# An mLSTM cell with a leaky-ReLU feed-forward on one core: the fourth w_in quarter narrowed ahead of step 5's scores, two q loads asked for first, six spare products

## The chip, the core and the metric

The kernel runs on one core of a Trainium2 chip. A core has a matrix engine (TensorE, PE in the profile, with its weight loads as PEld), a vector engine (VectorE, DVE), an activation engine (ScalarE, ACT), GpSimd (POOL) and SyncE (SP), which here only asks for DMA transfers. The metric is the device time of one execution in microseconds, lower is better; a time is the median of several runs.

## What is computed

```python
# q, k, v, o_gate: (4, 8, 768, 40) float32; i_gate, f_gate: (4, 8, 768)
for t in range(S):
    m_new = np.maximum(f_gate[:, :, t] + m, i_gate[:, :, t])
    f_stab = np.exp(f_gate[:, :, t] + m - m_new)
    i_stab = np.exp(i_gate[:, :, t] - m_new)
    m = m_new
    C = f_stab[:, :, None, None] * C + i_stab[:, :, None, None] * np.einsum('bhd,bhe->bhde', vt, kt)
    n = f_stab[:, :, None] * n + i_stab[:, :, None] * kt
    h_tilde = np.einsum('bhde,bhe->bhd', C, qt)
    nq = np.einsum('bhd,bhd->bh', n, qt)[:, :, None]
    denom = np.maximum(np.abs(nq), 1.0)
    y[:, :, t] = 1.0 / (1.0 + np.exp(-o_gate[:, :, t])) * h_tilde / denom
# (batch, head, seq, dim) -> x of (3072, 320); w_in (320, 2048), w_out (2048, 320)
h = x @ w_in
g = np.maximum(0.01 * h, h)
return (g @ w_out).astype(np.float32)
```

Both weights arrive as float64, so the kernel reads them as pairs of 32-bit words and narrows them to float32 itself.

## The kernel before

The sequence is cut into six chunks of 128 tokens. A step is one chunk of one of the four batches: step s is chunk s // 4, batch s % 4, so steps 0 to 3 are chunk 0, steps 4 to 7 chunk 1. Inside a chunk the recurrence is written as matrix products: scores of keys against queries, weighted by an exponential of gate sums, and a state carried from one chunk to the next. The feed-forward of a chunk runs on TensorE between the cell's products of the next chunk.

**The order is written out by hand** for TensorE, VectorE, ScalarE and GpSimd: the Python calls give each of these engines its queue in order. Each works its queue strictly in turn, so an instruction that waits holds up everything behind it on its engine. Only SyncE's queue is laid out by the planner.

**Chunk 0** is `first_chunk()`. It loads k, q, v and the output gates of steps 0 to 3, makes the scores (`u_scores`, sc), multiplies them into the weights w on VectorE (L594), forms the values (`u_values`, pa: 16 records of 41 columns for a step) and the gated output (`gate`), and transposes it into xT (`u_x`, xt). `warm(n)` (L346) is a helper that multiplies the identity by itself n times into a PSUM tile that nobody reads; chunk 0 begins with two such calls. The first two units of the feed-forward's first product (ph, L790) stand in the same function, the others in the loop behind it. All small PSUM tiles of chunk 0 and of the cell come from one pool of four buffers in turn (`psc`), those of the feed-forward from another four (`psf`).

**Weights.** w_in is loaded in four quarters (n = 0 to 3), w_out in eight blocks (n = 4 to 11) of 640 KB each (`load_weights`). Narrowing one takes six passes in a row: ScalarE L243 and L245, VectorE L247, ScalarE L251, VectorE L253 and L257 (`narrow_weights`; quarters 0 and 1 are done in halves by `narrow_part`, L273 to L287). `now` is a generator over the passes of n = 2 to 11, and the loop of chunk 1 takes a few of them at each index i.

**The loop of chunk 1** has 30 units of feed-forward work, of chunk 0's tokens: for i = 0 to 13 a first product of 256 tokens (ten pairs of records in ph, then its Prelu, L798, which frees its two PSUM banks); for i = 14 to 29 a quarter of an output product (po, L825), quarter m needing the w_out blocks 4 + 2m and 5 + 2m. Units 0 and 1 use w_in quarter n=0, 2 to 5 n=1, 6 to 9 n=2, and 10 to 13 the last quarter, n=3. Around these units `place` sets the cell's parts: for step 4 `u_parts` behind i=2 and `u_plain` behind i=5, for step 5 behind i=7 and i=10, for step 6 behind i=12 and i=15, for step 7 behind i=18 and i=21.

- `u_parts(s)`: transposes of the scaled q (`split_qs`, tq, L550), then the scores (sd, L644) and the state's update (L649) in turn; VectorE multiplies scores by w (L654), which needs the exponentials of `prep_exp` (ScalarE L488), and adds the state (L626).
- `u_plain(s)`: the output gate's tanh (L524), the values (hN, L695), denominators (L663 to L665), the gating (L706, POOL L711) and the second state update.
- `ahead(s)`, called behind the part before: `u_split(s)` transposes k and q of step s (tk, L564, copied by ScalarE at L570), then POOL scales q (`prep_qs`, L517), multiplies the state (L622) and scales k (`prep_vu`, L508). `prep_mask` (POOL L479) adds the mask to w, which a DMA has spread over the partitions (L437).
- `feed(s)` asks for k (L380), four pieces of v (L383) and two of w (L437); `load_late(s, 1)` for q and `load_late(s, 2)` for the output gate (L406, into the tiles rb, two in turn). `fetch` says behind which index the loads of w_out's later blocks (L229) are asked for.

Of the kernel before, what the change touches and what calls it, by code (L numbers as in the profile page):

```python
# [21 lines left out]
def kernel(  # L22
# [133 lines left out]
    def prepare_step(n):  # L156

        nc.gpsimd.memset(S_v[n][:SL, 0, :, :, DB:], 2.0)
        nc.gpsimd.memset(S_v[n][SL:, 1, :, :, DB:], 2.0)
        nc.gpsimd.memset(S_t[n][QW:SL, 1], 0.0)  # L160
# [240 lines left out]
    def load_late(s, i):  # L401

        if B <= s < 2 * B:
            if i > 0:
                c, b = divmod(s, B)
                nc.sync.dma_start(natural(s, i), (k, q, o_gate)[i][b, :, ts(c, P), :].rearrange("h p d -> p h d"))  # L406
        elif s < NS:
            load_blocks(s, i)
# [266 lines left out]
    def gate(s, eng=None):  # L675

        d = st[s]
        d["x"] = wk.tile([P, Dm], F32, name="x")
        x3 = d["x"][:].rearrange("p (h d) -> p h d", d=D)
        nc.vector.scalar_tensor_tensor(  # L680
            x3, in0=d["o"].rearrange("p (h d) -> p h d", d=D), scalar=1.0, in1=d["pa"][:, :, :D],
            op0=ALU.add, op1=ALU.mult,
        )
        (eng or nc.gpsimd).tensor_tensor(x3, x3, d["den"][:].unsqueeze(2).to_broadcast([P, H, D]), op=ALU.mult)
# [78 lines left out]
    def u_x(s, copy=nc.scalar.copy):  # L763

        c, b = divmod(s, B)
        d = st[s]
        if b == 0:
            st["xT", c] = wk.tile([P, KC, GT], F32, name="xT", bufs=1)
        xT = st["xT", c]
        xt = psc.tile([P, KF + 1, P], F32, name="xt", tag="c")  # L770
        for kk in range(KF):
            nc.tensor.transpose(xt[:, kk, :], d["x"][:, ts(kk, P)], ident[:])
        nc.tensor.transpose(xt[:KR, KF, :], d["x"][:, KF * P :], ident[:])
        tok = ts(b, P)
        copy(xT[:, :KF, tok], xt[:, :KF, :])
        copy(xT[:DP, KF + 1 :, tok], xt[DP:, :KF, :])
        copy(xT[DP:, KF : 2 * KF, tok], xt[:DP, :KF, :])
        copy(xT[:DP, KF, tok], xt[:DP, KF, :])
        copy(xT[DP:, 2 * KF, tok], xt[:DP, KF, :])
        if s >= B:  # L780
            del st[s]
# [108 lines left out]
    def feed(s):  # L890
        load(s)
        spread(s)

    def first_chunk():

        tensor_copy = nc.vector.tensor_copy
        for n in range(NL):
            nc.gpsimd.memset(S_t[n][:, 1, :, D:], 2.0)
            nc.gpsimd.memset(S_t[n][SL:, 0], 0.0)
        nc.scalar.activation(first[:], zeros[:], AF.Exp)  # L900
        nc.vector.tensor_copy(ident_b[:], ident[:])
        keys, values = slice(0, 2), slice(2, 3)
        load(0, keys)
        load(1, keys)
        load(0, values)
        load(1, values)
        load_o(0)
        load_o(1)
        load(2, keys)
        load(3, keys)  # L910
        load(2, values)
        load(3, values)
        load_weights(0, (0,))
        load_o(2)
        load_o(3)
        load_weights(1, (0,))
        warm(5)
        spread_mask(0)
        warm(2)
        gates(0)  # L920
        gates_exp(0)
        load_fi(2)
        bu, a, _ = bus[0]
        spread_first(a, 0)
        gates_T(0, bu)
        gates(1)
        run(prep_exp(0))
        u_transpose(0, tensor_copy)
        prep_vu(0)
        u_transpose(1, tensor_copy)  # L930
        u_scores(0)
        run(prep_exp(1))
        prep_vu(1)
        u_scores(1)
        u_state(0, tensor_copy)
        u_state(1, tensor_copy)
        gates_exp(1)
        prep_o(0)
        prep_o(1)
        spread_mask(2)  # L940
        spread_first(a, 2)
        run(prep_exp(2))
        load_weights(0, (1,))
        u_values(0)
        gate(0)
        u_values(1)
        gate(1)
        run(prep_exp(3))
        u_transpose(2)
        u_x(0, tensor_copy)  # L950
        u_scores(2)
        u_transpose(3, tensor_copy)
        u_x(1)
        prepare_step(0)
        prep_vu(2)
        prep_vu(3)
        load_weights(1, (1,))
        prepare_step(1)
        parts = [narrow_part(n, e) for n in range(2) for e in range(2)]
        u_scores(3)  # L960
        run(parts[0], 5)
        u_values(2)
        prep_o(2)
        prep_o(3)
        run(parts[0])
        gate(2, nc.vector)
        u_values(3)
        gate(3, nc.vector)
        run(parts[1], 5)
        ffs = ff_units(0)  # L970
        ffs[0]()
        u_x(2)
        run(parts[1])
        u_x(3, tensor_copy)
        u_state(2, nc.scalar.copy)
        u_state(3, nc.scalar.copy)
        run(parts[2], 1)
        ffs[1]()
        run(parts[2])
        u_gates(1)  # L980
        prepare_tiles()
        prepare_step(2)
        prepare_step(3)
        return ffs, parts[3]

    E = mybir.EngineType
    with tc.manual_schedule(engines={E.PE, E.DVE, E.Activation, E.Pool}):
        ffs, part = first_chunk()
        for s in (B, B + 1):
            feed(s)  # L990
            for i in range(1, 3):
                load_late(s, i)
            load_weights(s - B + 2)
        for n in range(3):
            load_weights(QN + n)
        for s in (B + 2, B + 3):
            feed(s)


        ffs = ffs[2:]  # L1000
        fetch = {5: (3, 4), 9: (5, 6), 16: (7,)}
        place = (2, 5, 7, 10, 12, 15, 16, 18, 21, 22, 24, 26, 28)
        late = {}
        masks = {0: (2, 3), 12: (4, 5)}
        pairs = (2, 2, 6, 6, 14, 14, 19, 19, 19)
        now = (None for n in range(2, QN + NF // 2) for _ in narrow_weights(n))
        for c in range(1, NB + 1):
            if c > 1:
                ffs = ff_units(c - 1)
            cells = cell_units(c) if c < NB else []  # L1010
            n_ff, n_c = len(ffs), len(cells)
            done = fed = 0
            waiting = []
            for i in range(n_ff):
                if c == 1:
                    run(now, (0, 0, 0, 3, 3, 0, 2, 2, 2)[i] if i < 9 else 3 if i < 14 else 4)
                    for n in fetch.get(i, ()):
                        load_weights(QN + n)
                for s, steps in lazy.items():
                    if s in late and late[s] > 0:  # L1020
                        late[s] -= 1
                    else:
                        run(steps, 3)
                for n in masks.get(i, ()) if 1 < c < NB else ():
                    if c * B + n < NS:
                        prep_mask(c * B + n)
                ffs[i]()
                if c == 1 and i == 0:
                    run(part)
                    prep_mask(B)  # L1030
                    ahead(B)
                    load_fi(3)
                if c + 1 < NB:
                    if i == (1 if c == 1 else 0):
                        gates(c + 1)
                    if i == (3 if c == 1 else 2):
                        gates_exp(c + 1)
                upto = min(n_c, sum(p <= i for p in (place if c == 1 else pairs)))
                while done < upto:
                    fn, s = cells[done]  # L1040
                    fn(s)
                    done += 1
                    if fn is u_mix:
                        waiting.append(s)
                    if fn is u_plain and s < 2 * B - 1 or fn is u_parts and s == 2 * B - 1:
                        ahead(s + 1)
                    elif fn is u_mix:
                        ahead(s + 2)
                    elif fn is u_plain:
                        prep_mask(s + 2)  # L1050
                        ahead(s + 2)
                if i >= n_ff // 2 - 1:
                    for s in waiting:
                        gather_x(s)
                    waiting.clear()
                while fed < done:
                    fn, s = cells[fed]
                    fed += 1
                    if fn in (u_mix, u_plain):
                        load_late(s + NR, 2)  # L1060
                        if s + NL < NS:
                            feed(s + NL)
# [31 lines left out]
```

## Time and profile before

| | us |
|---|---|
| median of 3 runs | 527.77 |
| lowest and highest | 527.13, 530.59 |
| the profiled execution | 527.16 |
| its span, first to last instruction | 525.3 |
| TensorE busy | 512.1 |
| VectorE, ScalarE, GpSimd busy | 204.9, 187.8, 108.1 |
| mean granted TensorE clock | 0.98 |

The span is cut by the page into 40 slices of 13.1 us. The digits are busy tenths; the row PEclk is the clock that TensorE was granted, in tenths. The row DMA shows the transfer engines:

```profile
DMA  9999968997635526575526665526532112000000
```

A group's row in the lists that follow gives the line, the engine, what is written and read, the number of instructions, the busy time and the idle time of the engine before them. A row of the timeline gives the start in us, the length, and in brackets the idle time before it with what ended it. A row of the chain of waits gives start, length and the work.

```profile
44.01 0.31 PE L564 MATMUL tk<-ident,kn 64*40 64x64 f32 x4
46.18 0.25 PE L564 MATMUL tk<-ident,rb 64*40 64x64 f32 x2 [1.86 <-DMA rb<-in_q_dram]
...
79.76 4.64 PE L790 MATMUL ph<-xT,w_in 64*128 64x256 f32 x20 [3.58 <-DVE w_in L257]
```

### The profile page before, as it was taken

The numbers are of one execution on the slowest core, as the hardware profiler recorded it, in microseconds if no ns is written. First come the engines' busy times: TensorE is split into PE (matmuls) and PEld (weight loads), VectorE is DVE, ScalarE is ACT, GpSimd is POOL, SyncE is SP. The second block draws the span as 40 slices with busy tenths as digits, with TensorE's granted clock in tenths as the row PEclk, the third lists the DMA queues.
The fourth block names the chain that finished last, engine by engine and source line by source line (L and its number), as shares of the span: only waits on it lengthen the run. The fifth ranks groups of instructions, "written<-read, shape, count | busy, mean of one in ns | idle before, by whom it ended". The sixth has DMA issues, their size and how long they took to land.

```text
span 525.3 us, 11276 instructions
## 1 busy us (share of the span) xinstructions
PE 512.1 (97%) x4495; PEld 333.1 (63%) x4495; DVE 204.9 (39%) x400; ACT 187.8 (36%) x477; POOL 108.1 (21%) x149
## 2 busy tenths in 40 slices
PE   8998979999999999999999999999999999999997
PEld 6787867777554577554577554577554577544674
DVE  6666434587039355039355039354037240000000
ACT  5568894977525122125112125112125100122100
POOL 4453223235005021026021026021013010000000
PEclk9878997999999999999999999999999999999999
DMA  9999968997635526575526665526532112000000
GB/s 122 147 190 164 239 142 200 197 165 152 164 72 117 137 72 159 133 153 119 133 74 151 136 136 130 135 82 160 126 89 64 46 44 87 14 0 1 12 12 25
DMA packets 164419, 59.12 MB, mean 113 GB/s; under 512 B 128432, under 2 KB 155632, under 8 KB 164368
## 3 DMA queue, kind: packets, MB, share of 16 engines
q1 hardware_dynamic: 163408, 56.31, 50.4%
q0 software_dynamic: 576, 1.97, 2.0%
q8 instruction: 35, 0.57, 0.5%
q10 hardware_dynamic: 384, 0.13, 0.1%
q14 instruction: 16, 0.13, 0.1%
HBM read 51.68 MB, written 6.70 MB: 111 GB/s over the span
## 4 chain that ended last, share of the span: by engine, by line
PE 87%; SPq 5%; DMA 3%; DVE 2%; ACT 1%; issue 1%; POOL 1%; ACTq 0%; POOLq 0%
PE po L825 40%; PE ph L790 38%; SPq L378 3%; PE pT L725 3%; PE sd L644 3%; DMA rb<-in_q_dram 1%; DMA acts<-in_moe_w_in_dram 1%; PE sd L649 1%; PE hN L695 1%; PE tk L564 1%; PE tq L550 1%; DVE w_in L257 1%; SPq L383 1%; DMA S<-in_v_dram 0%; SPq L392 0%
## 5 line engine op out<-in xcount | busy, mean ns | idle before, releaser
L790 PE MATMUL ph<-xT,w_in 64*128 64x512 f32 (+1 forms) x1120 | 220.4, 546 | 3.8 <-DVE w_in L257 3.6
L825 PE MATMUL po<-w_out,acts 128*128 128x320 f32 x768 | 211.1, 434 | 0.0
L825 PEld LDWEIGHTS po<-w_out,acts 128*128 128x128 f32 x768 | 144.4, 190 | 62.6 <-issue 3.8
L790 PEld LDWEIGHTS ph<-xT,w_in 64*128 64x128 f32 x1120 | 111.2, 194 | 98.5 <-issue 87.5
L798 ACT ACTIVATE acts<-ph 128x512 f32<-128x512 f32 (+1 forms) x112 | 53.6, 531 | 149.4 <-PE ph L790 149.4
L654 DVE TENSOR_TENSOR qn<-w,sd 64x512 f32<-64x512 f32 x40 | 27.4, 684 | 115.9 <-PE sd L649 61.5
L479 POOL TENSOR_TENSOR w<-w,i 128x512 f32<-128x512 f32 x20 | 27.8, 1394 | 120.8 <-DMA w<-a_dr 85.4
L622 POOL TENSOR_TENSOR S<-S,f 40x336 f32<-40x336 f32 x36 | 28.5, 792 | 115.0 <-PE pT L725 68.3
L488 ACT ACTIVATE w<-w,gT 128x64 f32<-128x64 f32 x160 | 41.2, 339 | 0.0
L833 ACT COPY y<-po 128x320 f32<-128x320 f32 x12 | 5.1, 425 | 84.2 <-PE po L825 84.2
L833 ACT COPY hn<-po 128x320 f32<-128x320 f32 x12 | 5.1, 425 | 76.9 <-PE po L825 76.9
L541 DVE TENSOR_TENSOR qn<-kqT,ea 64x512 f32<-64x512 f32 x32 | 27.0, 843 | 0.9
L732 DVE STREAM_TRANSPOSE hb<-pT 128x512 f32<-128x512 f32 x16 | 11.4, 714 | 39.1 <-PE pT L725 38.9
L739 POOL TENSOR_TENSOR xb<-xb,den 128x320 f32<-128x320 f32 x16 | 11.6, 727 | 66.7 <-DVE xb L736 66.7
L644 PEld LDWEIGHTS sd<-kqT 40*64 40x64 f32 x640 | 19.8, 135 | 6.1 <-issue 6.1
L644 PE MATMUL sd<-kqT 40*64 40x64 f32 x640 | 21.2, 220 | 0.0
L743 DVE STREAM_TRANSPOSE x<-xb 128x512 f32<-128x512 f32 x16 | 18.0, 1122 | 7.7 <-POOL xb L739 7.7
L535 DVE STREAM_TRANSPOSE kqT<-rb 128x512 f32<-128x512 f32 x32 | 20.4, 680 | 0.0
L649 PE MATMUL sd<-S,vu 64*40 64x42 f32 x576 | 20.1, 215 | 0.0
L649 PEld LDWEIGHTS sd<-S,vu 64*40 64x40 f32 x576 | 18.6, 111 | 0.0
L626 DVE TENSOR_TENSOR S<-S,sd 40x336 f32<-40x336 f32 x36 | 18.1, 503 | 1.0
L725 PEld LDWEIGHTS pT<-qn,S 128*64 128x64 f32 x512 | 15.6, 138 | 3.6 <-issue 3.5
(138 smaller groups left out, 348.4 us busy)
## 6 DMA issues: line engine op xcount, KB each, us to landing
w<-a_dr SPq DMA_DIRECT2D x40, 128.0 KB
rb<-in_k_dram SPq DMA_DIRECT2D x64, 80.0 KB
rb<-in_q_dram SPq DMA_DIRECT2D x64, 80.0 KB
rb<-in_o_gate_dram SPq DMA_DIRECT2D x64, 80.0 KB
ea<-a_dr SPq DMA_DIRECT2D x32, 128.0 KB
kn<-in_k_dram SPq DMA_DIRECT2D x24, 160.0 KB
raw<-in_moe_w_out_dram SPq DMA_DIRECT2D x6, 640.0 KB
S<-in_v_dram SPq DMA_DIRECT2D x80, 40.0 KB
```

Of the source, the lines that this page charges most:

```text
L479: nc.gpsimd.tensor_tensor(w, w, cm2.unsqueeze(1).to_broadcast([P, H, SL]), op=ALU.add)
L488: yield nc.scalar.activation(w[:, h, :], of, AF.Exp, bias=gT[c][:, 0, bh : bh + 1], scale=1.0)
L535: nc.vector.transpose(d["kqT"][:, i].rearrange("p (h t n) -> p h n t", n=TS, t=QW), raw_blocks(s, i, QW).rearrange("p (h n) d -> p h n d", ...
L541: nc.vector.tensor_tensor(mixed(s)[rows, 1 - r], d["kqT"][rows, 1].rearrange("p (h t) -> p h t", t=SL), d["ea"][rows], op=ALU.mult,)
L622: nc.gpsimd.tensor_tensor(new, old, g, op=ALU.mult)
L644: nc.tensor.matmul(bank[1 - u][toks, h, :], lhsT=kqT[rows, 0, ts(h, SL)], rhs=kqT[rows, 1, ts(h, SL)], start=True, stop=True,)
L649: nc.tensor.matmul(dC[u][:, h].rearrange("p k d -> p (k d)"), lhsT=d["ku"][toks, h], rhs=S_v[s % NL][toks, u, h, :, :V1], start=True, stop ...
L654: nc.vector.tensor_tensor(mixed(s)[toks, u], w[toks], bank[1 - u][toks], op=ALU.mult)
L725: nc.tensor.matmul(pT[DP * r : DP * (r + 1), j * P + u * SL : j * P + (u + 1) * SL], lhsT=S[:, u, h, :], rhs=m[:, u, h, :], start=True, st ...
L790: nc.tensor.matmul(ph[r][:, cols], lhsT=w_row(r, slot, j), rhs=xT[DP * r : DP * (r + 1), slot, cols], start=(slot == 0), stop=(slot == KC ...
L798: nc.scalar.activation(acts[:, f, cols], ph[r][:, cols], AF.Prelu, alpha=0.01)
L825: nc.tensor.matmul(po[n][:], lhsT=acts[:, f, ts(n, P)], rhs=w_out[:, f, :], start=(f == 0), stop=(f == NF - 1),)
```

## The change

Two calls of `warm` are put into chunk 0, four products ahead of step 3's scores and two between the values of steps 2 and 3. For steps 4 and 5 the q load goes ahead of k, v and w. In the loop of chunk 1 the passes of n=3 are taken three at a time at i = 6 and 7, where they were two at a time at i = 6, 7 and 8, and all later passes follow one index earlier; the loads in `fetch` at 9 and 16 move to 8 and 15.

```diff
         u_scores(2)
         u_transpose(3, tensor_copy)
         u_x(1)
+        warm(4)
         prepare_step(0)
...
         run(parts[0])
         gate(2, nc.vector)
+        warm(2)
         u_values(3)
         gate(3, nc.vector)
...
         for s in (B, B + 1):
+            load_late(s, 1)
             feed(s)
-            for i in range(1, 3):
-                load_late(s, i)
+            load_late(s, 2)
             load_weights(s - B + 2)
...
-        fetch = {5: (3, 4), 9: (5, 6), 16: (7,)}
+        fetch = {5: (3, 4), 8: (5, 6), 15: (7,)}
...
                 if c == 1:
-                    run(now, (0, 0, 0, 3, 3, 0, 2, 2, 2)[i] if i < 9 else 3 if i < 14 else 4)
+                    run(now, (0, 0, 0, 3, 3, 0)[i] if i < 6 else 3 if i < 14 else 4)
```

On VectorE this puts L253 and L257 of n=3 ahead of step 5's L654 and L626. On ScalarE it puts L243 and L245 of n=4 ahead of the Prelu of unit i=8, and so on for the later blocks. In SyncE's queue q of step 4 and of step 5 each moves up past seven entries, and two of the 640 KB loads of w_out, which had two pieces of k of step 9, the two of w of step 8 and one of ea (L445) between them, become neighbours.

## The prediction

> **What bounds the kernel now.** I read the page first: the busy digits by slice, the chain and the groups with their idle time. TensorE is busy in all of the span but a few places.
>
> ```profile
> PE   8998979999999999999999999999999999999997
> PEclk9878997999999999999999999999999999999999
> ```
>
> Every digit below 9, of busy share and of clock, lies in the first seven slices of 13.1 us, up to about 92 us. Behind them TensorE runs without a gap at full clock, so what the change is worth is how much earlier TensorE gets to the work at about 86 us. Next the chain of waits between 12 and 130 us:
>
> ```profile
> 39.31 6.82 DMA rb<-in_q_dram
> 46.18 1.09 PE tk L564 x60
> ...
> 76.13 0.69 DVE qn L654
> 76.85 0.50 DVE S L626
> 77.35 0.75 DVE w_in L253
> 78.12 1.50 DVE w_in L257
> 79.62 0.14 issue
> 79.76 4.64 PE ph L790 x20
> 84.40 1.30 PE hN L695 x32
> 85.70 1.03 PE tk L564 x64
> ```
>
> Two waits are seen: for step 4's q (its `u_split`, tk, starts at 46.18), and for the last w_in quarter (n=3), whose L253 and L257 stand on VectorE behind step 5's L654. That L654 waits for step 5's exponentials. From 79.76 on the chain is TensorE alone. Last, the windows of 1 us, for the clock (columns: stretch, length, busy of PE, PEld, DVE, ACT, POOL with counts, granted clock, DMA share, GB/s):
>
> ```profile
> 47.00:48.00 1.00, 1.00 (x21) 0.84 (x12) 0.86 (x2) 0.70 (x3) 1.00 (x2) 0.68 1.09 256
> 78.00:79.00 1.00, 0.00 (x0) 0.00 (x0) 0.96 (x2) 0.84 (x2) 0.00 (x0) 0.54 0.62 185
> 81.00:82.00 1.00, 1.00 (x6) 0.84 (x6) 0.49 (x1) 0.00 (x0) 0.00 (x0) 0.50 0.41 74
> 85.00:86.00 1.00, 1.00 (x49) 0.95 (x49) 0.19 (x2) 0.41 (x2) 0.17 (x1) 1.00 0.82 140
> ```
>
> After a gap the clock is half. Quarter-us windows put the half-clock stretches at 20.05 to 23.5, 30.3 to 37.1, 47.4 to 50.8 and 78.1 to 84.9: multiples of about 3.4 us on one grid. So the wait for w_in costs twice: 3.58 us of idle time (76.18 to 79.76), and 5.1 us of work at half clock (79.76 to 84.9), 2.6 us more.
>
> **Part 1: n=3's passes ahead of step 5's scores.** VectorE's queue becomes L247, L253, L257 (n=3), then L654 twice and L626. The last input of L257 is ScalarE's L251, which runs from 70.84 to 72.50; so L257 (1.50) ends at 74.0 instead of 79.6. Behind it wait L654 and L626 of step 5: L654 began at 75.42 for its exponentials (ScalarE L488, 74.80 to 75.39), so they lose nothing. What is late next is PSUM. Unit i=10 takes the two banks that unit i=8's Prelu (L798) frees. In the changed order ScalarE does n=4's L243 and L245 (0.77 and 0.93 us) ahead of that Prelu, which stood at 75.29; it moves to 76.9. The first bank is free at about 77.3, so unit 10 starts at 77.3, not 79.76. The gap of 1.1 us, with 1.5 us of matmuls ahead of it in the clock's stretch, I take not to drop the clock. Unit 10 at full clock is 2.36 us (the row of two units at 86.73, 4.52, shows the rate), hN 1.06 (row at 100.07): 80.8. There `u_split(6)` (tk) follows, at 85.70 in the trace.
>
> **It needs step 6's q.** SyncE asks for that at 77.44, and the trace's landing mark is 80.4. I find no wait on compute that would move it: from 60 to 69 us the queue is full of the w_in and w_out loads (390 GB/s at 65 to 67), from 69.4 to 77.4 it is one issue after another, some 0.6 us each. The change doesn't touch this part of the queue. So tk(6) can't start before about 80.5, whatever happens earlier: at most 5.2 us are to be had, and part 1 alone brings 85.70 - 80.8 = 4.9.
>
> **Part 2: q of steps 4 and 5 first.** q(4) is asked for at 29.8, behind the store of a, instead of 39.31. The wait before tk(4) goes (1.86 us in the PE row), and with it the half-clock stretch from 47.4 to 50.8 (3.4 us, costing 1.7). Moved past are k(4), four v loads and two w loads. w(4) lands later by q's own transfer, about 0.5 us (w's last mark 45.6, q's 46.1). POOL's mask(4) waits for w(4) (L479 at 45.81), behind it qs(4), the state and ku(4), done at 50.12; now 50.6. dC(4) needs ku(4), so the scores of step 4, at 54.2 before, come at 50.6 at best: 3.6 us earlier. Late next is the last piece of n=3's load, landing at 64.6, for which ScalarE's L243 (66.53) waits: only 1.9 us of the lead are left on ScalarE, the engine that is busy without a break from 66.5 to 78.8. Unit 10 then starts at 75.4, hN ends at 79.0, and tk(6) waits for q until 80.5. Worth on the path: 80.8 to 80.5, 0.3 us. q(5) moved past seven entries changes nothing: tk(5) had no wait.
>
> **Part 3: six spare products.** Each is two records of 128 columns; by the row of 16 records of 320 columns in 4.50 us, 0.11 us each at full clock, so 0.9 us for four and 0.45 for two. The four lie in the gap of 1.19 us before step 3's scores (26.49, VectorE L581): hidden. The bank they take is the one step 2's scores freed at 25.24. The two stand between pa(2) and pa(3). Cover: the first w_in pass (L287) ends at 32.31, pa(3) at 32.19. If the clock still drops at 30.3, four records of pa slip into the slow part, 0.45 + 4 x 0.13 = 1.0 us, 0.12 of it covered, and the unit begun at 32.36 ends 0.6 us later; if they keep the clock up, that unit (4.64 us) takes 2.4: 2.2 us earlier. Both ends are swallowed by w(4) at 50.6 and q(6) at 80.4, so I take 0.
>
> The Trainium skill ("TensorE: Matmul & The Clock Gate", Why this matters for your kernels) says that gaps up to about 3 us between bursts keep the clock. That speaks against the spare products: the gap of 1.19 us would need no filling. The trace is harsher. The gap from 44.25 to 46.18, 1.9 us, was followed by half clock, and the stretch at 30.3 followed no gap at all but the pa products of 41 columns. By the page the waits left after the change (about 1.4 us before tk(6)) cost no clock, and the sum is -5.2; by the trace a gap near 1.9 us costs one stretch, 3.4 us at half, and it is -3.5. I take the page's side for 1.4 us, since the 1.2 us gap at 25.3 passed, and keep the other as a rival.
>
> **Part 4: later passes and loads one unit earlier.** Two 640 KB loads, at 96.92 and 100.26, become neighbours; w(8), ea(9) and a piece of k(9) land some 2 us later, and their users stand beyond 120 us. The last block of w_out (n=11) is nearest to the path: its L257 ends at 128.53, its first product starts at 129.76. With TensorE 5 us ahead it is wanted at 124.8. Its load lands at 119.9 in the trace, then L243, L245, L251 and L257 (0.8 + 0.9 + 0.9 + 0.8) give 123.4. Between nothing and 1.2 us; I take 0.2.
>
> **Sum.** -4.9 (part 1), -0.3 (part 2), 0, +0.2: -5.0. The profiled execution took 527.16 (span 525.3 and 1.9 around it): 522.2. The median of the runs is 0.6 above it, and the runs spread to 530.6; with half of that 0.6, **522.5 us**.
>
> **Rivals.**
> - *The clock drops in front of q(6).* For it: 1.9 us sufficed at 44 us. One stretch at half, +1.7: about 524.2.
> - *q(6) lands earlier.* The chain names POOL's ku(5) (L508, 67.60) as releasing a v load on SyncE. If that wait is real, it ends about 2 us earlier, and so does q(6), then hN at 79.0 decides, 1.4 us before 80.5: 521.1. Against it: the same third v load was held up behind the full queue at 31.86, too.
> - *The last w_out blocks give it back.* VectorE reached L257 of n=11 only at 127.3, 7 us after the load. If its queue, not the load, sets that, TensorE waits at the last quarter of the output products: 526 to 527, no change.
> - *Slower.* Unit 8 waits for unit 6's Prelu, unit 10 for unit 8's, tk(6) for q: three gaps of 1 to 2 us between 67 and 80.5. If each spoils its stretch, the clock stays at half from 67.8 until a whole busy stretch, after 85. Nine us of work from unit 8 to tk(6) take 18, and tk(6) ends at 86.5, as before, with two more us at half behind it: +1, 528.5. It decides if two stretches running hold less than half their time in dense matmuls.
>
> **How the numbers follow.** Main case 0.52, clock drop 0.18, earlier q 0.14, given back 0.10, slower 0.06. The likeliest gives 522.5. A change of 1% is 5.3 us (522.5), about what a measurement of this kernel tells from no change: the main case lies on that edge. Half of it and the earlier q give 0.42 for faster, 0.54 within; of the slower case and what I overlook 0.04 lies beyond 1%. The range of 520.3 to 525.6 takes in the main case with 1 us on either side, the earlier q and the clock drop, and leaves out the last two.
>
> **What would show it.** L257 of n=3 ends before step 5's L654, near 72 to 74; no PE wait on it. tk(4) follows its predecessor at once, tk(6) starts within 0.3 us of q(6)'s landing at 80.4, with a PE wait on the q load there; unit 10's weight load waits on ScalarE. Full clock from 47 to 81. I am wrong if q(6) lands before 79.5 or after 81.5, or TensorE waits again after 90 us.

## The result, and the profile after

| | before | after |
|---|---|---|
| median of 18 runs, us | 527.49 | 526.80 |
| lowest and highest, us | 526.16, 532.88 | 524.40, 532.32 |
| the profiled execution, us | 527.16 | 524.40 |
| its span, us | 525.3 | 522.5 |
| TensorE busy, us | 512.1 | 509.1 |
| mean granted TensorE clock | 0.98 | 0.99 |

The ratio of the runs, after to before, is 0.9974, with a 95% interval of 0.9953 to 0.9996: 1.4 us faster (0.7 by the medians), where 5.0 were forecast. The ratio leaves out one slow run of after, the one of 532.32 us. The time, 526.8, lies outside the predicted range. The profiled execution of after is the fastest of its 18 runs, so its trace shows the change from its good side: 2.8 us of span less, twice what the runs give.

The page of after, its busy and clock digits:

```profile
PE   8989987999999999999999999999999999999997
PEclk9889999999999999999999999999999999999999
```

The dips near 48 and 80 us are gone from the clock row. The granted clock is half only from 19.7 to 23.1 and from 33.3 to 36.8 us. The lowest busy digit ahead of the last slice, the 7, is the slice from 78 to 91 us. VectorE's timeline of after says that the passes went where the change puts them, L257 of n=3 ahead of step 5's L654:

```profile
71.11 1.49 DVE L257 CUSTOM_DVE_ANT_0 w_in<-w_in,raw 128x2560 uint16<-128x2560 uint16 x1 [2.88 <-ACT raw L251]
74.00 1.40 DVE L654 TENSOR_TENSOR qn<-w,sd 64x512 f32<-64x512 f32 x2 [1.39 <-ACT w L488]
```

L257 ends at 72.6 instead of 79.6. TensorE's timeline has what comes instead of that wait:

```profile
75.87 2.70 PE L790 MATMUL ph<-xT,w_in 64*128 64x256 f32 x20 [1.12 <-ACT acts L798]
82.75 0.25 PE L564 MATMUL tk<-ident,rb 64*40 64x64 f32 x2 [2.88 <-DMA rb<-in_q_dram]
```

Unit 10 waits 1.1 us for unit 8's Prelu, and step 6's `u_split` waits 2.9 us for its q. It starts at 82.75; in the prediction's chain of before it started at 85.70. That difference, 2.9 us, is the whole change of the span (2.8), since behind it TensorE has no wait over 0.25 us up to 200 us. The chain of waits of after, in the stretch that ends there (columns: start, length, work; rows of issue and rows under 0.1 us are left out between):

```profile
74.79 0.64 SPq L383
75.47 0.64 SPq L383
76.21 0.60 SPq L383
77.34 0.60 SPq L383
78.04 0.58 SPq L437
78.67 0.85 SPq L437
79.62 3.10 DMA rb<-in_q_dram
82.75 1.09 PE tk L564 x60
83.85 4.52 PE ph L790 x40
```

In the prediction's view of before the chain ran over VectorE's passes at this place. Now it runs over SyncE: one issue after another (SPq), v and w of step 7, and at their end q of step 6. It is asked for at 79.62 and has landed at 82.71; before it was asked for at 77.44 and had landed at 80.44. The load that the forecast had taken as fixed came 2.3 us later.

### The profile page after: what moved, and what is told of

The parts are those of the page before. It is cut to its first block, busy times and chain, and to the rows that moved or that the text cites. A ratio compares the mean times of both kernels' runs of the same rounds, so it can differ in the third digit from the quotient of the medians.

```text
span 522.5 us, 11302 instructions
## 1 busy us (share of the span) xinstructions
PE 509.1 (97%) x4507; PEld 331.1 (63%) x4507; DVE 205.3 (39%) x400; ACT 187.6 (36%) x477; POOL 106.9 (20%) x149
## 3 DMA queue, kind: packets, MB, share of 16 engines
q1 hardware_dynamic: 163408, 56.31, 50.1%
## 4 chain that ended last, share of the span: by engine, by line
PE 89%; SPq 5%; DMA 2%; ACT 2%; issue 1%; DVE 1%; ACTq 0%; DVEq 0%
PE po L825 40%; PE ph L790 39%; SPq L378 3%; PE pT L725 3%; PE sd L644 3%; DMA acts<-in_moe_w_in_dram 1%; PE sd L649 1%; PE tk L564 1%; PE hN L695 1%; DMA rb<-in_q_dram 1%; PE tq L550 1%; SPq L383 0%; SPq L392 0%; ACT kqT L570 0%; PE tg L357 0%
## 5 line engine op out<-in xcount | busy, mean ns | idle before, releaser
L790 PE MATMUL ph<-xT,w_in 64*128 64x512 f32 (+1 forms) x1120 | 216.5, 537 | 3.5 <-ACT acts L798 1.9
L790 PEld LDWEIGHTS ph<-xT,w_in 64*128 64x128 f32 x1120 | 108.6, 189 | 97.5 <-issue 87.7
L654 DVE TENSOR_TENSOR qn<-w,sd 64x512 f32<-64x512 f32 x40 | 27.4, 684 | 106.7 <-PE sd L649 58.6
L626 DVE TENSOR_TENSOR S<-S,sd 40x336 f32<-40x336 f32 x36 | 18.1, 503 | 1.0
```

The source lines that it names most:

```text
L654: nc.vector.tensor_tensor(mixed(s)[toks, u], w[toks], bank[1 - u][toks], op=ALU.mult)
L790: nc.tensor.matmul(ph[r][:, cols], lhsT=w_row(r, slot, j), rhs=xT[DP * r : DP * (r + 1), slot, cols], start=(slot == 0), stop=(slot == KC ...
```

## The experiments

My theory after the result: with the w_in wait gone, TensorE is held by SyncE's stream of loads, and the change itself makes that stream later, by asking for q of steps 4 and 5 first. The rival: q(6) is only the first of several waits, so the gain is given back wherever the next one is, and the order of the q loads is harmless. All ratios are to the kernel before, run alongside on the same chip, with the 95% interval.

**q of step 6 asked for earlier, in the changed kernel and in the kernel before.** The calls that ask for k, v and w of steps 6 and 7 come later in the program, and so q(6) moves up by eleven entries in SyncE's queue.

```diff
-        for s in (B + 2, B + 3):
-            feed(s)
...
                     ahead(B)
+                    for s in (B + 2, B + 3):
+                        feed(s)
```

> The changed kernel with one more edit: q of step 6 is asked for eleven entries earlier (ahead of the later v and w pieces of step 6 and all of step 7). My theory: in the changed kernel step 6's transposes wait for this load (2.9 us in its profile), and that wait takes back the gain. Then q(6) lands some 6 us earlier, the wait before tk(6) is gone, tk(6) starts at about 79.7 instead of 82.7 us, and the time is 3 us or more under the changed kernel's: ratio to the kernel before about 0.990 or less. Rival (the transfers as a whole are the bound, whatever their order): the wait moves to v or w of steps 6 and 7, and the ratio stays at 0.997. Rival (the clock's drops vary from run to run and make up the difference): the wait goes but the ratio stays.

> The kernel before with q of step 6 asked for eleven entries earlier, nothing else. My theory: in the kernel before nothing waits for q(6), since the last w_in quarter holds TensorE until 85.7 us; so no change, ratio 0.999 to 1.001. Rival (the transfers' order is worth something by itself): 0.995 or less.

Measured: 1.0003 (0.9983 to 1.0023) for the changed kernel with the edit, 1.0007 (0.9991 to 1.0023) for the kernel before with it. In the first, q(6) lands at 73.9 and its wait is gone. TensorE's timeline of that run shows what takes its place:

```profile
98.96 0.33 PE L564 MATMUL tk<-ident,rb 64*40 64x64 f32 x2 [3.59 <-DMA rb<-in_q_dram]
```

That is step 7's q, which landed at 98.91, and half clock followed from 98.0 to 104.8. Half of my theory holds (the wait on q(6) can be moved away), but this order within SyncE's queue only makes the next q the late one, and no time is won. In the second kernel the w_in wait is there as before:

```profile
79.35 3.90 PE L790 MATMUL ph<-xT,w_in 64*128 64x256 f32 x20 [3.58 <-DVE w_in L257]
```

**The parts alone.** The passes and their loads alone (the `fetch` and `run(now, ...)` lines of the change, which no run takes apart), the q order and the spare products without the passes, the passes with the spare products, and the passes with the q order.

> The kernel before with the passes of n=3 and the two fetches earlier, without the q loads of steps 4 and 5 moved and without the spare products. My theory: part 1 alone takes away the wait for w_in (3.6 us) and the half clock behind it, and unit 10 waits for unit 8's Prelu instead; TensorE comes to step 6's transposes at about 80.8 us and waits for q(6) there. The ratio is then as good as the whole change's, 0.993 to 0.998. Rival (the q loads and the spare products carry the gain): no wait for w_in, but 0.999 or more.

> The changed kernel with the passes of n=3 and the fetches put back: only the q loads of steps 4 and 5 and the spare products are left. My theory: TensorE reaches the last w_in quarter earlier and waits there for it longer (some 5 us instead of 3.6), so the ratio is 0.998 to 1.001. The rest lead of ScalarE's queue, at most 1.9 us, is the most that can be left: 0.996. Rival (these parts carry the gain): 0.997 or less.

> The passes and fetches with the six spare products, without the q loads moved. My theory: the spare products change nothing that lasts, since TensorE waits for step 4's q at 46 us in either case: the ratio of the passes alone, 0.993 to 0.996. Rival (the spare products cost what the whole change lost against the passes alone): 0.997 or more.

> The passes and fetches with the q loads of steps 4 and 5 moved ahead, without the spare products. Theory: moving q ahead puts back w(4), n=2's load, k(5), v(5) and w(5) (in the profiles with q first, w(5) lands at 57 to 59 us, without it at 55 to 56.8) and opens a gap before q(6) in which the clock can drop; so this is the part that takes back what the passes gain: 0.996 to 0.999. Rival (it is neutral, and the spread between the runs is the clock's): 0.993 to 0.996.

| passes early | q(4), q(5) first | spare products | ratio | 95% interval |
|---|---|---|---|---|
| yes | | | 0.9945 | 0.9926 to 0.9964 |
| yes | | yes | 0.9928 | 0.9900 to 0.9956 |
| yes | yes | | 0.9985 | 0.9971 to 1.0000 |
| | yes | yes | 1.0023 | 1.0004 to 1.0041 |
| yes | yes | yes | 0.9974 | 0.9953 to 0.9996 |

The q order costs: 0.9985 against 0.9945, intervals apart, some 2.1 us of 527.5. The passes are worth 2.9 us (1 - 0.9945), or with the other two parts there 2.6 (0.9974 / 1.0023). The spare products are worth between nothing and 0.9 us; the intervals overlap. In the profile with them TensorE comes to the wait for q(4) at 41.98 instead of 44.25 and is released at 45.76 instead of 46.17, so most of that lead of 2.3 us is waited away there. As a product, 0.9945 x (0.9985 / 0.9945) x (0.9928 / 0.9945) = 0.9968, near the 0.9974 of the whole.

TensorE's timelines at the wait for q(6): passes alone first, with its wait for q(7) below, then passes with the q order.

```profile
81.52 0.25 PE L564 MATMUL tk<-ident,rb 64*40 64x64 f32 x2 [0.27 <-DMA rb<-in_q_dram]
98.27 0.25 PE L564 MATMUL tk<-ident,rb 64*40 64x64 f32 x2 [1.03 <-DMA rb<-in_q_dram]
```

```profile
86.44 0.33 PE L564 MATMUL tk<-ident,rb 64*40 64x64 f32 x2 [3.89 <-DMA rb<-in_q_dram]
```

Passes alone, TensorE reaches the place at 81.25 and waits a quarter of a microsecond, and again 1.0 at q(7). With the q order q(6) lands at 86.40. Without the passes the wait for w_in is there in full, and longer than before, as that load is late too:

```profile
81.64 4.64 PE L790 MATMUL ph<-xT,w_in 64*128 64x256 f32 x20 [4.53 <-DVE w_in L257]
```

**q(6) and q(7) asked for by GpSimd**, whose own scaling of the q before (L517) is what frees the tile rb, so that it waits for no other engine there. (Each of the two issues takes GpSimd about 0.95 us in these profiles.)

```diff
-                nc.sync.dma_start(natural(s, i), (k, q, o_gate)[i][b, :, ts(c, P), :].rearrange("h p d -> p h d"))
+                (nc.gpsimd if i == 1 and s >= B + 2 else nc.sync).dma_start(natural(s, i), (k, q, o_gate)[i][b, :, ts(c, P), :].rearrange("h p d -> p h d"))
```

> The passes and fetches alone (as in the run of the passes only), and q of steps 6 and 7 asked for by GpSimd instead of SyncE, right behind the scaling of the q that stood in the same tile. My theory: with the w_in wait gone, TensorE is held by SyncE's stream of loads: in the passes-only run it waits 0.3 us for q(6) and 1.0 us for q(7), more in runs with a slower stream. With both loads off that stream the two waits go, and the entries behind come one or two issues earlier: a ratio of 0.990 to 0.993, against 0.9945 with the passes alone. GpSimd's two issues (some 0.7 to 1.3 us each) stand ahead of the scaled k and cost nothing at step 5, up to 0.5 us at step 4. Rival (the passes have given all they can; the rest is the clock): 0.994 to 0.996.

> The changed kernel with q of steps 6 and 7 asked for by GpSimd instead of SyncE. My theory: TensorE waits 2.9 us for q(6) in the changed kernel, and as much for q(7) once q(6) is early. With both gone the lead of the first 80 us stays: a ratio of 0.988 to 0.992, 3 us or more under the changed kernel. Next late would be the last w_out block. Rival (the stream as a whole is the floor): another wait for the stream, a w_out block or v, takes its place, and the ratio stays at 0.996 or more.

> Passes of n=3 early, spare products in, q(4) and q(5) in their old place, q(6) and q(7) asked for by GpSimd. My theory (TensorE is held by SyncE's stream of loads; spare products are worth 0 to 0.2%): ratio 0.985 to 0.990 to the kernel before, no wait on q(6) or q(7), the wait for q(4) at 42 to 46 us still there. The rival (the spare products do nothing, or the 0.9885 of the version without them was a lucky series): 0.989 to 0.995.

> The kernel before with q(6) and q(7) asked for by GpSimd and nothing else. My theory (q(6) is not what TensorE waits for there, the w_in pass is): ratio 0.998 to 1.001, the wait on w_in L257 before 80 us of 3 to 4.5 us still there. The rival (two issues fewer in SyncE's queue are worth by themselves what they brought to the passes, 0.6%): 0.992 to 0.996.

| q(6), q(7) by GpSimd, in | ratio | 95% interval |
|---|---|---|
| the passes alone | 0.9885 | 0.9854 to 0.9917 |
| the passes with the spare products | 0.9887 | 0.9849 to 0.9925 |
| the changed kernel | 0.9938 | 0.9918 to 0.9957 |
| the kernel before | 0.9988 | 0.9971 to 1.0004 |

With the passes it takes the waits for q(6) and q(7) away and brings another 0.6%; the medians, 523.18 us against 528.57 for the kernel before in the same series, make it 0.5%. It is six runs only, but the six with the spare products agree. It beats both kernels. In the kernel before the same edit brings nothing that can be told from no change, so it is not the shorter SyncE queue by itself. There TensorE still waits for w_in ahead of that place:

```profile
78.72 3.91 PE L790 MATMUL ph<-xT,w_in 64*128 64x256 f32 x20 [3.58 <-DVE w_in L257]
```

In the changed kernel half of the gain is missing again: the q order costs 0.5% here too, though no q is waited for. Its profile shows another path to TensorE: the last part of n=3's own load lands at 69.8 (65.1 in after), ScalarE idles for it, the Prelu behind is late, and TensorE waits 3.8 us, with half clock from 72.2 to 79.0. ScalarE's timeline, then TensorE's:

```profile
69.85 1.36 ACT L243 ACTIVATE w_in<-raw 128x1280 f32<-128x1280 f32 x1 [4.07 <-DMA raw<-in_moe_w_in_dram]
74.02 9.33 PE L790 MATMUL ph<-xT,w_in 64*128 64x256 f32 x60 [3.80 <-ACT acts L798]
```

So the wait for q(6) is one place where the late queue reaches TensorE, and not the only one. The spare products add nothing here (0.9887 against 0.9885). TensorE's timeline of the passes alone with this edit shows what is late next, a transpose behind VectorE's L706, which stands behind w_out's passes:

```profile
102.57 0.28 PE L352 MATMUL tg<-ident,bu 32*128 32x32 f32 x2 [3.20 <-DVE hn L706]
```

**Which q load it is.** The passes with only q(4) moved ahead of its k, v and w, with only q(5), with q(4) moved past its two w loads alone, and last the passes and spare products with q of all four steps 4 to 7 asked for by GpSimd.

```diff
         for s in (B, B + 1):
+            if s == B:
+                load_late(s, 1)
             feed(s)
-            for i in range(1, 3):
+            for i in range(2 if s == B else 1, 3):
                 load_late(s, i)
```

(The second has `s > B` in place of `s == B`; in the third the added lines stand between the two calls of `feed`, the loads of k and v and those of w.)

> Passes of n=3 early and only q(4) asked for ahead of its k, v and w. My theory (q(4) is issued while the queue is full and pushes k(4), v(4), w(4) and all behind them back): the last w(5) lands at 57.5 to 60 us and q(6) at 83 to 86, ratio 0.997 to 0.9995, no wait before tk(4). The rival (it is q(5) that does it): w(5) at 55 to 56.5, q(6) near 81.5, ratio 0.993 to 0.996.

> Passes of n=3 early and only q(5) asked for ahead of its k, v and w. My theory (the move of q(4) is what slows the stream): w(5) lands at 55 to 57 us, q(6) near 81.5 to 82.5, ratio 0.993 to 0.996, the wait before tk(4) of 1 to 2 us still there. The rival (it is q(5)): w(5) at 57.5 to 60, q(6) at 83 to 86, ratio 0.997 to 0.9995.

> Passes of n=3 early, q(4) asked for ahead of w(4) only, behind k(4) and v(4). Theory A (what costs is that k(4) and v(4) are pushed behind the stall of 5 us at 32 to 37 us): the two issues there are as in the kernel before, w(5) lands at 55 to 56.5 us, ratio 0.993 to 0.996, the wait before tk(4) shorter by 0.5 to 1.3 us. Theory B (any earlier q(4) costs): w(5) at 57.5 us or later, ratio 0.997 to 0.9995.

> Passes of n=3 early, spare products in, q of all four steps 4 to 7 asked for by GpSimd (q(4) and q(5) near 34 us, behind its w_in loads). Theory A (what costs is the place in SyncE's queue ahead of k(4), v(4), w(4)): the wait before tk(4), 2.2 us without this, goes, w(5) lands by 56 us, ratio 0.982 to 0.988. Theory B (q(4)'s transfer itself, moved ahead of the second half of chunk 1's loads, is what delays them): w(5) lands at 57.5 us or later and the ratio is 0.989 to 0.994, no better than with q(6) and q(7) alone.

Measured: 0.9989 (0.9971 to 1.0007) with q(4) first, 0.9938 (0.9911 to 0.9965) with q(5) first, 0.9978 (0.9961 to 0.9994) with q(4) ahead of w alone. So it is q(4) that costs, and q(5) is free, as the forecast had said of it. (The interval of q(4) ahead of w alone just touches those of the passes alone and of q(5) first.) TensorE's timelines at q(6), q(4) first, then q(5) first, then q(4) ahead of w alone:

```profile
84.25 0.33 PE L564 MATMUL tk<-ident,rb 64*40 64x64 f32 x2 [3.63 <-DMA rb<-in_q_dram]
```

```profile
81.37 0.25 PE L564 MATMUL tk<-ident,rb 64*40 64x64 f32 x2 [1.32 <-DMA rb<-in_q_dram]
```

```profile
84.16 0.25 PE L564 MATMUL tk<-ident,rb 64*40 64x64 f32 x2 [3.52 <-DMA rb<-in_q_dram]
```

The run with q(4) ahead of w alone went against my theory A, that only a place ahead of k(4) and v(4) costs: two entries suffice. w(5) landed at 56.9 there and at 57.0 with q(5) first, so that mark, which I had chosen to tell the cases apart, doesn't. With all four q asked for by GpSimd the ratio was 0.9891 (0.9832 to 0.9951), no better than with two; the interval takes in both theories, and its profiled execution, at 530.1 us the longest of its six, is not used for landings.

What does tell them apart is how the first half of w_in's third quarter (n=2) lands. A load has 16 landing marks; these are its first and last, in us, in all the other profiles:

| q(4) at its old place | first, last | q(4) asked for earlier | first, last |
|---|---|---|---|
| before | 48.5, 48.7 | after | 48.7, 50.5 |
| before, q(6) early | 48.8, 49.6 | after, q(6) early | 49.1, 51.2 |
| passes | 48.6, 48.9 | no passes | 50.3, 52.1 |
| passes, q by GpSimd | 48.9, 49.4 | after, q by GpSimd | 49.5, 54.0 |
| passes, spare products | 48.2, 48.7 | passes, q order | 48.9, 51.9 |
| the same, q by GpSimd | 46.7, 47.7 | passes, q(4) first | 48.9, 50.2 |
| before, q by GpSimd | 49.3, 49.7 | passes, q(4) ahead of w | 49.8, 51.0 |
| passes, q(5) first | 47.8, 48.5 | | |

The first marks overlap (46.7 to 49.3 and 48.7 to 50.3). The last come 0.2 to 1.1 us behind the first on the left, and 1.2 to 4.6 on the right: some of the 16 parts are late, and no last mark of one side lies within the other's. In each of these profiles one of the v loads of step 5 behind it stays in issue until 0.5 to 1.6 us past that last mark: in after its first v is in issue from 47.11 to 51.18, 0.7 us past it. The windows of 52 to 56 us show the transfers that are then missing (columns: stretch, length, busy of PE, PEld, DVE, ACT, POOL, clock, DMA share, GB/s); before, then after:

```profile
52.00:56.00 4.00, 4.00 (x116) 3.45 (x114) 0.00 (x0) 2.83 (x10) 0.90 (x1) 1.00 0.76 161
```

```profile
52.00:56.00 4.00, 4.00 (x44) 3.56 (x39) 1.67 (x3) 3.93 (x8) 0.00 (x0) 1.00 0.53 63
```

The transfer engines move 63 GB/s there instead of 161 (136 with the passes alone, 36 with both q loads added; with q(4) and with q(5) alone 105 and 106, so this row does not tell those two apart). Why an earlier q(4) spreads the parts of a later load, no run shows.

## Why the prediction was wrong

- **The failed step** is "The change doesn't touch this part of the queue. So tk(6) can't start before about 80.5", with part 2's costing of the entries that q(4) is moved past. I had read SyncE's queue from 60 to 77 us as fixed, since it has no wait on compute, and given the reorder 0.5 us on w(4). But in these profiles the queue inherited the lateness of the loads ahead: w(4)'s last mark went from 45.6 to 46.5, n=2's from 50.1 to 52.1, w(5)'s from 54.9 to 58.0, the third w_out block's from 69.6 to 71.5, q(6)'s from 80.4 to 82.7. Part of it may belong to chunk 0, which varies: SyncE's last load of w_in in chunk 0 is asked for at 28.5 us in before and at 29.4 in after, and between 28.0 and 29.7 in the nine profiles whose chunk 0 is that of before. It is not the whole: two profiles with q(4) in its old place have that load at 29.7, and n=2's last mark there, 49.6 and 49.7, is still ahead of every one with q(4) early. Part 2 was forecast at -0.3 us net; the runs give +2.1.
- **Part 1** had the mechanism right: L257 at 72.6 (72 to 74 forecast), unit 10 behind unit 8's Prelu, the 1.1 us gap harmless to the clock. With the passes alone L257 ends at 74.0 and unit 10 starts at 77.25, where the forecast had 74.0 and 77.3 (VectorE's row, then TensorE's):

```profile
72.47 1.49 DVE L257 CUSTOM_DVE_ANT_0 w_in<-w_in,raw 128x2560 uint16<-128x2560 uint16 x1 [2.88 <-DMA S<-in_v_dram]
77.25 2.69 PE L790 MATMUL ph<-xT,w_in 64*128 64x256 f32 x20 [1.13 <-ACT acts L798]
```

Its size was 4.9 us (its own terms, 77.3 + 2.36 + 1.06, give 80.7 and 5.0). Alone, the passes are worth 2.9 (1.9 to 3.9), the second term that was off. In their profile tk(6) starts at 81.52, 4.2 us earlier, and 1.0 us goes at q(7): a wait behind 90 us, which the forecast had excluded once TensorE was ahead. With q(6) and q(7) asked for by GpSimd the passes reach 5 to 6 us, so the lead was there and SyncE's queue took it. The measured terms, -2.9, +2.1 and 0 to -0.9 for part 3, make a gain of 0.8 to 1.7 us; 1.4 was measured.
- **q(5)** was right: moved past seven entries it costs nothing.
- **The wait before tk(4)** went as forecast, in after, and with it the half clock at 47 us. It was worth nothing: q(4) early in any of three ways brought no gain, and the forecast had given it only 0.3 us.
- **Part 3**, taken at 0, holds: 0 to 0.9 us.
- **The clock before q(6).** The gap was 2.9 us, twice the 1.4 allowed for, and cost no clock. That was luck of where it lay in the clock's grid (last section). The rival of a clock drop in front of q(6) did not come true here. It did in kernels with gaps of 3.5 to 3.9 us at that place.
- **The rivals.** "q(6) lands earlier" had the sign wrong. "The last w_out blocks give it back" named the right size (no change at 526 to 527) and the wrong place: no wait behind 90 us in after. "Slower" did not come: the clock stays full from 36.8 to 521 us. The condition "I am wrong if q(6) lands ... after 81.5" is the one that was met.
- **The range** took a landing mark of one profiled execution for the landing. In the profiles of before, the passes alone, with the spare products and with q(5) first, q(6) landed at 80.4, 81.5, 82.2 and 81.3; TensorE, there by 81, stands or falls with such differences, and the main case had 1 us for them.
- **Two slips that change nothing.** The last slice of the row PE, a 7, is below 9 too; it is the end of the kernel and the same after. Half of the main case and the earlier q are 0.40, not 0.42.

## What to carry to other kernels

A queue of issues without waits on compute is not fixed: a load put ahead in it can make later ones late (here q(4), 160 KB, did and q(5), of the same size, did not), so cost a moved load at the end of the queue and not at its neighbours. When a compute wait is removed in front of a load that lands within a microsecond of it, ask who issues that load: here handing two q loads to GpSimd, which frees their tile itself, turned 0.55% into 1.15% (1.0% by the medians). Test the parts of a change alone, since one of three can eat most of what another brings.

## What the hardware showed that I had not expected

**Which gaps cost the clock.** In every profile the changes of the clock lie on one grid of 3.41 us, whose place differs from run to run; the Trainium skill ("TensorE: Matmul & The Clock Gate", Part 1, What's actually happening) calls it a free-running window of 3413 ns, and the traces agree. It is the idle time within one such stretch that decided, in all but one case. The windows of after, cut on its grid (the second to fourth columns of numbers are busy PE, PEld, DVE):

```profile
77.71:81.12 3.41, 2.16 (x43) 1.60 (x40) 2.85 (x7) 2.17 (x5) 1.52 (x3) 1.00 0.50 105
81.12:84.53 3.41, 1.77 (x67) 1.62 (x69) 0.72 (x2) 0.64 (x2) 2.00 (x4) 1.00 0.57 114
84.53:87.94 3.41, 3.41 (x34) 3.08 (x32) 0.82 (x1) 3.35 (x8) 1.85 (x2) 1.00 0.58 150
```

The gap of 2.9 us is split by the grid into 1.25 and 1.63 us of idle time, and both following stretches keep the full clock. In the profile of the passes alone a gap of 1.92 us lies within one stretch, and the next has half:

```profile
43.26:46.68 3.42, 1.50 (x48) 0.99 (x48) 2.38 (x5) 2.85 (x6) 0.77 (x1) 1.00 0.92 137
46.68:50.09 3.41, 3.41 (x52) 2.82 (x42) 3.27 (x4) 2.61 (x6) 3.25 (x4) 0.50 1.13 215
```

All sixteen profiles were cut so. Behind chunk 0, every stretch at full clock with 1.86 us of idle time or more was followed by half, and those up to 1.63 were not, but for one with 1.45 us. Once at half, a stretch with 0.9 us or more of idle time was followed by another at half. So one gap costs more in one run than in the next: the wait for w_in, 3.58 us long in the profile of before and in two others with its order of passes (before with q(6) early, before with q by GpSimd), was followed by 6.8 us at half in the first and 3.4 in the other two. In chunk 0 stretches with no idle time, filled for the most part with the products of 41 columns, were followed by half clock too (26.87 to 30.29 in before). The page's rule for kernels (Why this matters for your kernels), that gaps up to about 3 us are safe, holds for the gap of 2.9 us here and not for those of 1.9.

**Late parts of a load.** The 16 marks of one 384 KB load (the first half of n=2), within 0.2 to 1.1 us of each other with q(4) in its old place, spread to 4.6 us in one profile with it early, and an issue behind it stayed open until after the last.
